# Twelve short fp32 dummy matmuls for six long ones at the start, and one expert-weight load moved behind the last eb loads (Fourier layer and soft MoE, one core)

## The chip, the cores and the metric

The kernel runs on one core of a Trainium2 chip. The metric is device time in microseconds, the median of several runs. Names of engines: PE is TensorE's matrix engine and PEld its weight loading, DVE VectorE, ACT ScalarE, POOL GpSimd, SP SyncE, which here only issues DMAs.

## What is computed

Input `x` is 8 sequences of 2496 tokens with 256 features. A Fourier layer with soft thresholding is followed by a soft mixture of 8 experts with 4 slots each, all in fp32:

```python
X = np.fft.rfft(x, axis=1); Xr, Xi = X.real, X.imag
Yr = Xr @ w_r - Xi @ w_i + b_r
Yi = Xr @ w_i + Xi @ w_r + b_i
Yr = np.sign(Yr) * np.maximum(np.abs(Yr) - 0.01, 0)     # Yi alike
y = np.fft.irfft(Yr + 1j * Yi, n=2496, axis=1).reshape(19968, 256)

logits = y @ phi                                        # phi 256 x 32
d = softmax(logits, over the 19968 tokens)
slot_input = (d.T @ y).reshape(8, 4, 256)
slot_out[e] = np.maximum(slot_input[e] @ w1[e], 0) @ w2[e]   # w1 256 x 1024, w2 1024 x 256
out = softmax(logits, over the 32 slots) @ slot_out
```

## The kernel before

The transforms are matmuls with constant matrices, in two factors of the sequence length. A batch (one of 8 sequences) goes through short groups on PE (pa and px for the forward transform, pk and py for the complex weights, pt, pr and further ones behind the threshold), and its dispatch logits, weights and slot sums follow some groups later. The whole program is written by generators in a heap: each yields a time, and what is due first is written first. Times of the tail are relative to `TB` (function `at`). What is written goes onto its engine in that order: `sp()` (L243) issues a DMA from SP, `aq()` from ACT's queue, `mm()` (L249) and `tr()` (L634) write matmuls and transposes on PE, and each keeps program order. A helper's line is thus the line of many instructions.

**The head.** While the first inputs travel (`xf`, which holds transform constants and the first rows, and the `x` tiles), PE runs dummies: a tile `warm` of zeros, 128x128, multiplied into the PSUM tile `wps`, which nothing reads (L293 to L297). It is an F32R tile, an fp32 form in which a matmul is a single pair of weight load and matmul here. Behind them `head()` (L450) writes the q matmuls (`q_mm`, L394), plain fp32, whose results are copied to `at` and `atr`. The layer's weights come as `wri`, of which POOL and ACT derive sums and differences (`wsum`, `wdh`).

**The tail.** For batch 7 `last_chain()` (L1040) does what the other batches have behind them already: `pg` gives dispatch logits, which ACT copies to `g_sb` and sends to the DRAM tile `gd` (`aq`); SP reads them back in another layout as `gp` (`sp`), and PE multiplies them into `L` (`pL`). Then come the dispatch weights: `ed` is their DRAM tile, `eb` what is read back from it, for batch 6 as for batch 7, and `pd` the slot sums. The combine's logits are read back as `cin` from `c_dr` (`c_load`, L1161), split to `chl` on POOL (`c_prep`), and multiplied by `pc` on PE (`c_trans`, L1180). The experts run in between: `mlp1` with `w1`, `mlp2` with `w2` into `po` (L1222 to L1246). In the last stage `pq` makes the result, ACT and DVE copy it to `ost`, and SP sends it out (L1297 to L1336).

**The expert weights.** 32 matrices of 512 KB (16 of `w1`, 16 of `w2`) have no room of their own. The table `PLAN["T_"]["wl"]` (L156) lists for each, in order, when it is loaded and into which room: `load_w` (L933) takes the next matrix of `wlist`, so that the i-th entry is the i-th matrix. Rooms are tiles whose first use is over: `r`, `a`, `q`, `sm`, `xs` in the chain's pools, `t` one of the `ta_tile` tiles, `h` half an `hl` tile, `hx` one tile more, `T` two of the transposed tiles. `x` is a pair of half matrices (128x512 each), one in a tile of tag `xth` and one of tag `xtl`; each tag has three buffers (`chain_bufs`, L207). Each half is one DMA of SP.

Of the kernel before, what the change touches and what calls it, by code (L numbers as in the profile page):

```python
# [12 lines left out]
F32 = mybir.dt.float32  # L13
F32R = mybir.dt.float32r
# [40 lines left out]
def _constants():  # L55
# [97 lines left out]
    "ko": 0.915,  # L153
    "to": 0.7,
    "late": {'6': {'cms': [11.5, 19.69, 854.1, 854.2, 854.2, 854.2], 'eb': 21.015, 'pt': ['pl', 'pf'], 'de': 0.005, 'pd': [30.6, 30.61], 'pr': [31.55, 31.6, 31.65, 31.7, 31.75], 'pL': [6.05, 6.5], 'pm': 8.05, 'mo': 0.1, 'pb': 9.05, 'eo': 0.4, 'pe': [11.1, 11.5], 'pg': [0.875, 1.275], 'fr': {'sinv': 0, 'm2': 0, 'f1': 0, 'suni': 0}}, '5': {'cms': [14.3, 14.8, 15.6, 20.0, 20.8, 21.5], 'pg': [1.1, 1.8], 'pL': [6.5, 7.2], 'pm': 8.52, 'de': 0.68, 'mo': 0.1, 'pb': 9.05, 'eo': 0.1, 'fr': {'sinv': 1, 'm2': 1, 'f1': 1, 'suni': 0}, 'pe': [11.35, 12.35], 'pp': [12.05, 12.6], 'pd': [18.9, 19.3], 'pr': [40.2, 40.21, 40.22, 40.23, 40.24]}, '4': {'pr': [18.4, 20.49, 24.49, 28.49, 32.49]}},
    "T_": {'wl': [[-45, 'r'], [-44, 'r'], [-43, 'r'], [-31.0, 't'], [-30.7, 't'], [-29.4, 't'], [-27.6, 't'], [-27.8, 't'], [-25, 'q'], [-23.5, 'q'], [-11, 'a'], [-10.3, 'a'], [-9.6, 'a'], [-9.45, 'sm'], [-9.4, 'xs'], [-8.31, 'x'], [-8.3, 'x'], [-8.29, 'x'], [1.07, 'h'], [1.07, 'h'], [13.55, 'h'], [13.55, 'h'], [13.55, 'h'], [13.55, 'h'], [13.55, 'hx'], [13.61, 't'], [13.61, 't'], [13.61, 't'], [13.61, 't'], [13.61, 't'], [13.7, 'T'], [13.7, 'T']], 'cl': 1.02, 'cp': 46.5, 'ct': 46.6, 'du': [[-4.5, 0], [-2.4, 0], [1.2, 0]], 'd1': [5, 2, 4, 0, 0, 0], 'cm': [19.9, 19.91, 19.92, 25, 25.1, 25.2], 'cm7': [0.1, 0.12, 0.3, 0.4, 1, 1], 'ye': 0.2, 'te': [[5.6, 0.2], [5.5, 0.4]], 'pg': [-7, -6.4965, -6.458], 'yt': 0.5, 'wr': -30.6, 'tp': {-2: [0, 0.9, 1.05, 1.05], -1: [-2.4975, -2.497, -2.46, -2.459]}, 'tt': [[[-6.4605, -6.44], -0.3, -0.25, -0.2, [-6.5, -6.4585]], [0.6, 0.7, 0, 0, 0], [12, 11.45, 12.2, 12.3, 12.4]], 'tg': {(7, 0): ('pt', 'ps'), (5, 4): ('ps', 'pl'), (5, 0): ('pl', 'ps')}, 'eg': {(6, 2, 1): 'A', (6, 4, 0): 'V', (6, 4, 1): 'A'}, 'z': 13.55, 'th': [0.1, 0.12], 'tl': [0.2, 0.25]},  # L156
    "f1": [1.5, 2.4],
    "ap1": 1.9,
    "f0": 0.2,
# [29 lines left out]
def fourier_soft_moe_kernel(ctx: ExitStack, tc: tile.TileContext, t: dict, out: bass.AP):  # L189
# [21 lines left out]
    def psum(tag, name):  # L211
        return pp.tile([128, 512], F32, tag=tag, name=name, bufs=psum_bufs[tag])

    def wtile(shape, dt, tag, name):
        if tag == "rte":
            return wqp.tile(list(shape), dt, tag=tag, name=name, bufs=2)
        if tag in a_bufs:
            return wap.tile(list(shape), dt, tag=tag, name=name, bufs=a_bufs[tag])
        if tag in main_bufs:
            return wmp.tile(list(shape), dt, tag=tag, name=name, bufs=main_bufs[tag])  # L220
        return wcp.tile(list(shape), dt, tag=tag, name=name, bufs=chain_bufs[tag])

    x = t["x"]
# [6 lines left out]
    V, A, P = (_InOrder(tc, e) for e in (nc.vector, nc.scalar, nc.gpsimd))  # L230
# [18 lines left out]
    def mm(**kw):  # L249
        tc.keep_in_program_order(nc.tensor.matmul(**kw))  # L250
# [39 lines left out]
        x0.append([xf[:P1, Q1 + e * D : Q1 + e * D + D] for e in range(GP)])  # L290
        pools["f1x"] = xf[:P1, :Q1].rearrange("p (c a r) -> p c a r", c=2, r=R)

    warm = wtile([128, 128], F32R, "k1", "warm")  # L293
    P.memset(warm.bitcast(F32), 0.0)
    wps = psum("ps", "wps")
    for _ in range(6):
        mm(out=wps, lhsT=warm, rhs=warm.unsqueeze(1).broadcast_to([128, 4, 128]), start=True, stop=True)  # L297

    while len(x0) < G // GP:
        load_x0()  # L300
# [11 lines left out]
    xs = wtile([128, 6 * KS], F32R, "xs", "xs")  # L312
# [721 lines left out]
    T_ = PLAN["T_"]  # L1034
# [173 lines left out]
    rhs = []  # L1208
# [98 lines left out]
    for j in range(NBLK):  # L1307
# [6 lines left out]
        if not pqs:  # L1314
            pqs = [(k, psum(("pf", "pl")[k % 2], f"pq{k}")) for k in ((0, 1) if j == 0 else (j,))]
            for a in range(2):
                for k, pq in pqs:
                    lo = k * TR - k * TR % F
                    mm(
                        out=pq,  # L1320
                        lhsT=cts[lo][:, k * TR - lo : k * TR - lo + TR],
                        rhs=rhs[a].rearrange("p b d -> p (b d)"),
                        start=(a == 0),
                        stop=(a == 1),
# [4 lines left out]
        if j + 1 == starts[i] + OUTS[i]:  # L1329
            n = OUTS[i] * 512  # L1330
            sp(
                out=out[128 * 512 * starts[i] : 128 * 512 * (j + 1)].rearrange("(p f) -> p f", p=128),
# [68 lines left out]
```

## Time and profile before

| | us |
|---|---|
| runs | 517.89, 517.67, 515.95 |
| median | 517.67 |
| profiled execution, its own time | 516.78 |
| span of that execution, first to last instruction | 515.0 |
| PE busy in the span | 500.7 (97%) |
| DVE, ACT, POOL busy | 405.7, 312.6, 296.2 |
| result leaves (last stage) | from 461.89 on |

The span is a little shorter than the time of the execution that it belongs to; the rest lies before the first and behind the last instruction. Matmuls are pipelined, so that the busy time of PE is the time in which some matmul is under way. What stood still and for whom is read from the timeline, where a row has the idle time ahead of it and what ended that, and from the chain of work that ended last. The DMA share counts the time of packets on the 16 DMA engines; queue q1 holds SP's DMAs, q10 ACT's, q8 the fetches of PE's instructions.

### The profile page before, as it was taken

What the parts mean: (1) busy time and instruction counts of PE and PEld (TensorE: products, weight loads), DVE (VectorE), ACT (ScalarE), POOL (GpSimd) and SP (SyncE); (2) the same over time, 40 slices, a digit from 0 to 9 for tenths busy, and PEclk for the clock granted to TensorE, in tenths of its full rate; (3) what the DMA queues carried; (4) which work ended last, traced back from release to release, by engine and by line L of the source; (5) the groups of instructions that cost most, each with busy time, mean ns of one, the idle gap of its engine ahead of it and who ended that gap; (6) DMA issues with size and microseconds to landing.
All of it is one profiled execution on the core that took longest, in us unless ns stands there. A gap on an engine that the chain in (4) does not pass through costs nothing.

```text
span 515.0 us, 11951 instructions
## 1 busy us (share of the span) xinstructions
PE 500.7 (97%) x4475; PEld 440.1 (85%) x4475; DVE 405.7 (79%) x776; ACT 312.6 (61%) x704; POOL 296.2 (58%) x280
## 2 busy tenths in 40 slices
PE   8999999999999999999999999999999999999992
PEld 7889999999999999998999898889899878468881
DVE  2897787799968898889889988897898866257661
ACT  2776666777676766676667666655534446138761
POOL 0686786768676757675667577867475503153310
PEclk9999999999999999999999999999999999999997
DMA  8655555675665657565656566696685567959998
GB/s 299 229 186 185 182 171 201 177 242 149 257 181 183 165 194 203 175 167 201 188 174 174 211 186 207 163 307 182 242 256 150 199 163 194 410 198 403 408 419 342
DMA packets 87485, 114.91 MB, mean 223 GB/s; under 512 B 46191, under 2 KB 65119, under 8 KB 85891
## 3 DMA queue, kind: packets, MB, share of 16 engines
q1 hardware_dynamic: 86860, 113.65, 66.5%
q8 instruction: 35, 0.57, 0.5%
q10 hardware_dynamic: 567, 0.50, 0.3%
q14 instruction: 23, 0.19, 0.1%
HBM read 66.78 MB, written 47.34 MB: 222 GB/s over the span
## 4 chain that ended last, share of the span: by engine, by line
PE 84%; DMA 6%; DVE 4%; POOL 1%; ACT 1%; issue 1%; SPq 1%; DVEq 0%; ACTq 0%; POOLq 0%
PE py L250 21%; PE px L250 13%; PE pk L250 10%; PE pa L250 10%; PE pq L250 9%; PE pt L634 6%; PE pr L250 3%; PE pe L250 2%; PE pc L1186 2%; PE pL L250 2%; PE pg L250 2%; PE pd L250 1%; PE hps L250 1%; DMA out<-ost 1%; DMA gp<-gd 1%; DMA wri<-in_w 1%
## 5 line engine op out<-in xcount | busy, mean ns | idle before, releaser
L185 POOL TENSOR_TENSOR xs<-xsm,xs 128x256 fp32r<-128x256 f32 x77 | 63.3, 823 | 96.4 <-DVE xs L185 66.3
L185 POOL TENSOR_TENSOR rt<-ut,rt 128x512 f32<-128x512 f32 x79 | 104.7, 1326 | 15.1 <-DVE rt L185 13.8
L185 POOL TENSOR_TENSOR xl<-xr,xh 117x512 fp32r<-117x512 f32 x72 | 97.7, 1357 | 12.9 <-ACT xh L185 12.9
L250 PE MATMUL px<-smov,ap 128*128 128x128 f32 x640 | 85.1, 276 | 0.1
L250 PEld LDWEIGHTS px<-smov,ap 128*128 128x128 f32 x640 | 80.3, 192 | 4.8 <-DVE xsm L185 0.3
L185 DVE SCALAR_TENSOR_TENSOR ut<-py,pk,k 128x256 f32<-128x256 f32 x160 | 69.5, 475 | 11.7 <-PE py L250 11.0
L185 ACT CAST xth<-px 128x512 fp32r<-128x512 f32 x80 | 46.9, 587 | 43.6 <-PE px L250 21.6
L185 ACT COPY ast<-pa 128x512 f32<-128x512 f32 x75 | 44.2, 589 | 46.1 <-PE pa L250 46.1
L185 DVE TENSOR_TENSOR xtl<-px,xth 128x512 fp32r<-128x512 f32 x80 | 54.6, 683 | 18.6 <-ACT xsm L185 18.6
L250 PE MATMUL pk<-xs,w_rh 128*128 128x256 f32 (+1 forms) x320 | 66.1, 290 | 0.1
L185 DVE TENSOR_SCALAR rt<-ut 128x512 f32<-128x512 f32 x69 | 65.5, 949 | 0.6
L250 PE MATMUL py<-xth,nwsh 128*128 128x256 f32 (+1 forms) x160 | 53.2, 333 | 0.1
L250 PEld LDWEIGHTS pk<-xs,w_rh 128*128 128x128 f32 x320 | 51.9, 189 | 0.9 <-DVE xs L185 0.6
L185 ACT CAST xh<-xr 117x512 fp32r<-117x512 f32 x75 | 47.4, 635 | 0.4 <-DMA xr<-in_x 0.4
L634 PE MATMUL pt<-pk,rt 128*128 128x128 f32 x320 | 45.2, 274 | 0.0
L250 PE MATMUL py<-xth,wdh 128*128 128x256 f32 (+1 forms) x160 | 44.8, 280 | 0.0
L250 PE MATMUL py<-xtl,nwsh 128*128 128x256 f32 (+1 forms) x160 | 44.6, 279 | 0.0
L250 PE MATMUL py<-xtl,wdh 128*128 128x256 f32 (+1 forms) x160 | 44.5, 278 | 0.0
L250 PE MATMUL py<-xth,wdl 128*128 128x256 f32 (+1 forms) x160 | 44.5, 278 | 0.0
L250 PE MATMUL py<-xth,nwsl 128*128 128x256 f32 (+1 forms) x160 | 44.4, 278 | 0.0
L250 PE MATMUL pk<-xs,w_rl 128*128 128x256 f32 (+1 forms) x160 | 44.4, 278 | 0.0
L185 ACT COPY T<-pt 128x512 f32<-128x512 f32 x66 | 39.2, 601 | 6.8 <-PE pt L634 5.1
(197 smaller groups left out, 1192.3 us busy)
## 6 DMA issues: line engine op xcount, KB each, us to landing
xr<-in_x SPq DMA_DIRECT2D x35, 512.0 KB
ap<-adr SPq DMA_DIRECT2D x70, 256.0 KB
adr<-ast SPq DMA_DIRECT2D x21, 768.0 KB
out<-ost SPq DMA_DIRECT2D x12, 1024.0 KB
w<-in_moe_w SPq DMA_DIRECT2D x21, 512.0 KB
out<-ost SPq DMA_DIRECT2D x14, 512.0 KB
hl<-in_moe_w SPq DMA_DIRECT2D x6, 512.0 KB
x<-in_x SPq DMA_DIRECT2D x10, 256.0 KB
```

Of the source, the lines that this page charges most:

```text
L185: return lambda *a, **k: self.tc.keep_in_program_order(f(*a, **k))
L250: tc.keep_in_program_order(nc.tensor.matmul(**kw))
L634: tc.keep_in_program_order(nc.tensor.transpose(out=out, in_=in_, identity=identity))
L1186: nc.tensor.transpose(out=pc[:, i * P1 : (i + 1) * P1], in_=chls[b][x][:, 2 * (r + i) : 2 * (r + i) + 2].rearrange("p g h s -> p (g h s)") ...
```

## The change

It has two parts. In the head `warm` is a plain F32 tile, and twelve matmuls of 64 columns are written where six of 512 were. In the table the third `x` entry leaves its place at -8.29 (the 18th entry) and a new one stands at 13.56, behind `hx` (the 25th). As entries are matched to matrices by place, the matrices 17 to 24 change rooms with that: 17 and 18 go to `hl` halves, 19 to 22 to the next `hl` halves, 23 to `hx`, 24 to the `x` pair; the others keep theirs.

```diff
-    "T_": {'wl': [ ... [-8.31, 'x'], [-8.3, 'x'], [-8.29, 'x'], [1.07, 'h'], [1.07, 'h'], [13.55, 'h'], ... [13.55, 'hx'], [13.61, 't'], ...
+    "T_": {'wl': [ ... [-8.31, 'x'], [-8.3, 'x'], [1.07, 'h'], [1.07, 'h'], [13.55, 'h'], ... [13.55, 'hx'], [13.56, 'x'], [13.61, 't'], ...
...
-    warm = wtile([128, 128], F32R, "k1", "warm")
-    P.memset(warm.bitcast(F32), 0.0)
+    warm = wtile([128, 128], F32, "k1", "warm")
+    P.memset(warm, 0.0)
     wps = psum("ps", "wps")
-    for _ in range(6):
-        mm(out=wps, lhsT=warm, rhs=warm.unsqueeze(1).broadcast_to([128, 4, 128]), start=True, stop=True)
+    for _ in range(12):
+        mm(out=wps[:, :64], lhsT=warm, rhs=warm[:, :64], start=True, stop=True)
```

On PE, at the program's start, this is the row of matmuls before; `q_0` and `q_1` are the first two PSUM tiles of `q_mm`, and an fp32 matmul, one row here, is two pairs in the trace:

```order
L1397 UNCONDITIONAL_BRANCH
L250 MATMUL wps<-warm 128x512 x6
L250 MATMUL q_0_150<-xf 128x2x20x3 x2
L250 MATMUL q_1_153<-xf 128x2x20x3 x2
L250 MATMUL q_0_150<-xf,x_2_89 128x2x20x3 x2
```

and with the change:

```order
L1397 UNCONDITIONAL_BRANCH
L250 MATMUL wps<-warm 128x64 x12
L250 MATMUL q_0_156<-xf 128x2x20x3 x2
L250 MATMUL q_1_159<-xf 128x2x20x3 x2
L250 MATMUL q_0_156<-xf,x_2_95 128x2x20x3 x2
```

The number of dummies and their size differ; what follows on PE is the same.

On SP, at the old place of the third `x` load (at 411 us in the trace), before: `w_0` and `w_1` are the two halves of a matrix, `ed` the dispatch weights of batch 6, `gp` the logits of batch 7 read back:

```order
L244 DMA w_0_6241<-in_moe_w 128x512
L244 DMA w_1_6242<-in_moe_w 128x512
L244 DMA w_0_6249<-in_moe_w 128x512
L244 DMA w_1_6250<-in_moe_w 128x512
L244 DMA ed_6256<-ea_6169 120x704
L244 DMA gp_6417<-gd_6271 40x22x32 x2
L244 DMA gp_6417<-gd_6271 40x20x32
```

and with the change:

```order
L244 DMA w_0_6247<-in_moe_w 128x512
L244 DMA w_1_6248<-in_moe_w 128x512
L244 DMA ed_6258<-ea_6175 120x704
L244 DMA gp_6419<-gd_6273 40x22x32 x2
L244 DMA gp_6419<-gd_6273 40x20x32
```

One pair of halves is gone ahead of `ed`.

On SP, at the new place, before (`eb` of batch 7, then the `hl` halves, `hx` as the first `w`, and the first of the five loads into `ta_tile` tiles):

```order
L244 DMA eb_6627<-ed_6498 64x20x32 x2
L244 DMA hl_6632<-in_moe_w 128x1024 x2
L244 DMA hl_6635<-in_moe_w 128x1024 x2
L244 DMA w_6638<-in_moe_w 128x1024
L244 DMA w_6650<-in_moe_w 128x1024
```

and with the change:

```order
L244 DMA eb_6629<-ed_6500 64x20x32 x2
L244 DMA hl_6634<-in_moe_w 128x1024 x2
L244 DMA hl_6637<-in_moe_w 128x1024 x2
L244 DMA w_6640<-in_moe_w 128x1024
L244 DMA w_0_6652<-in_moe_w 128x512
L244 DMA w_1_6653<-in_moe_w 128x512
L244 DMA w_6656<-in_moe_w 128x1024
```

The two halves stand between `hx` and the `ta_tile` loads. The order on DVE, ACT and POOL is the same; on PE the `mlp2` matmuls of the shifted matrices read other tiles.

## Rows read from the trace of the kernel before

**Rows 1.** The page, parts 1, 3, 4: engines; a queue; chain shares

```profile
PE 500.7 (97%) x4475; PEld 440.1 (85%) x4475; DVE 405.7 (79%) x776; ACT 312.6 (61%) x704; POOL 296.2 (58%) x280
...
q8 instruction: 35, 0.57, 0.5%
...
PE 84%; DMA 6%; DVE 4%; POOL 1%; ACT 1%; issue 1%; SPq 1%; DVEq 0%; ACTq 0%; POOLq 0%
```

**Rows 2.** Windows: us, PE, PEld, DVE, ACT, POOL, PEclk, DMA share, GB/s

```profile
460.00:462.00 2.00, 1.72 (x8) 1.42 (x8) 1.06 (x3) 0.92 (x3) 1.09 (x1) 1.00 0.04 8
...
464.00:466.00 2.00, 2.00 (x13) 1.65 (x12) 1.78 (x4) 1.75 (x5) 1.50 (x2) 1.00 1.03 410
```

**Rows 3.** Timeline, head: start us, us, instruction, count [idle before <-releaser]

```profile
0.99 2.93 PE L250 MATMUL wps<-warm 128*128 128x512 f32 x6 [0.99 <-POOL warm L185]
...
4.46 1.15 PE L250 MATMUL q<-xf 117*128 117x120 f32 x8 [0.54 <-DMA xf<-in_xf]
...
6.63 7.22 PEld L250 LDWEIGHTS q<-xf,x 117*128 117x128 f32 x64 [0.31 <-DMA x<-in_x]
...
16.48 0.62 ACT L185 CAST wdh<-wri 128x512 fp32r<-128x512 f32 x1 [0.35 <-POOL wri L185]
```

**Rows 4.** Chain of work that ended last, the head: start us, us, what

```profile
7.93 5.43 DMA wri<-in_w
...
22.39 0.70 PE pa L250 x3
```

**Rows 5.** Windows, columns as in rows 2: PE behind pL

```profile
424.86:441.70 16.84, 16.81 (x187) 12.87 (x184) 11.06 (x24) 9.15 (x20) 5.33 (x10) 1.00 0.80 245
```

**Rows 6.** Timeline of SP's DMA issues, about 411 us

```profile
410.82 0.37 SPq L244 DMA_DIRECT2D w<-in_moe_w  x1
411.29 0.38 SPq L244 DMA_DIRECT2D w<-in_moe_w  x1
411.76 0.39 SPq L244 DMA_DIRECT2D ed<-ea  x1
```

**Rows 7.** DMA queues: packets, MB, share; 413 to 415, then 415 to 417

```profile
q1 hardware_dynamic: 304, 0.59, 85.8%
q10 hardware_dynamic: 2, 0.00, 0.4%
...
q10 hardware_dynamic: 403, 0.31, 46.5%
...
q8 instruction: 1, 0.02, 3.0%
```

**Rows 8.** Chain of work that ended last, 415 to 424 us

```profile
415.85 2.83 DMA gd<-g_sb
...
419.74 3.58 DMA gp<-gd
```

**Rows 9.** Timeline of PE, 420 to 425 us

```profile
421.22 1.97 PE L634 MATMUL pt<-pk,rt 128*128 128x128 f32 x16
423.45 1.41 PE L250 MATMUL pL<-gp,pk 120*117 120x352 f32 x4 [0.26 <-DMA gp<-gd]
```

**Rows 10.** Timeline of SP's DMA issues: three of the five last cin reads

```profile
449.20 0.33 SPq L244 DMA_DIRECT2D cin<-c_dr  x1
450.51 0.30 SPq L244 DMA_DIRECT2D cin<-c_dr  x1
...
452.50 0.30 SPq L244 DMA_DIRECT2D cin<-c_dr  x1
```

**Rows 11.** Timeline of all engines, 454 to 463 us

```profile
454.91 3.64 PE L250 MATMUL po<-w,z 128*32 128x256 f32 x64
...
456.82 0.62 POOL L185 CAST chl<-cin 117x512 fp32r<-117x512 f32 x1
...
461.89 1.17 SPq L244 DMA_DIRECT2D out<-ost  x2
...
462.25 0.56 PE L1186 MATMUL pc<-pk,chl 117*128 117x117 f32 x4
```

More of the change, by code (lines that the diff above doesn't have):

```diff
@@ L155 @@
     "late": {'6': {'cms': [11.5, 19.69, 854.1, 854.2, 854.2, 854.2], 'eb': 21.015, 'pt': ['pl', 'pf'], 'de': 0.005, 'pd': [30.6, 30.61], 'pr': [31.55, 31.6, 31.65, 31.7, 31.75], 'pL': [6.05, 6.5], 'pm': 8.05, 'mo': 0.1, 'pb': 9.05, 'eo': 0.4, 'pe': [11.1, 11.5], 'pg': [0.875, 1.275], 'fr': {'sinv': 0, 'm2': 0, 'f1': 0, 'suni': 0}}, '5': {'cms': [14.3, 14.8, 15.6, 20.0, 20.8, 21.5], 'pg': [1.1, 1.8], 'pL': [6.5, 7.2], 'pm': 8.52, 'de': 0.68, 'mo': 0.1, 'pb': 9.05, 'eo': 0.1, 'fr': {'sinv': 1, 'm2': 1, 'f1': 1, 'suni': 0}, 'pe': [11.35, 12.35], 'pp': [12.05, 12.6], 'pd': [18.9, 19.3], 'pr': [40.2, 40.21, 40.22, 40.23, 40.24]}, '4': {'pr': [18.4, 20.49, 24.49, 28.49, 32.49]}},
-    "T_": {'wl': [[-45, 'r'], [-44, 'r'], [-43, 'r'], [-31.0, 't'], [-30.7, 't'], [-29.4, 't'], [-27.6, 't'], [-27.8, 't'], [-25, 'q'], [-23.5, 'q'], [-11, 'a'], [-10.3, 'a'], [-9.6, 'a'], [-9.45, 'sm'], [-9.4, 'xs'], [-8.31, 'x'], [-8.3, 'x'], [-8.29, 'x'], [1.07, 'h'], [1.07, 'h'], [13.55, 'h'], [13.55, 'h'], [13.55, 'h'], [13.55, 'h'], [13.55, 'hx'], [13.61, 't'], [13.61, 't'], [13.61, 't'], [13.61, 't'], [13.61, 't'], [13.7, 'T'], [13.7, 'T']], 'cl': 1.02, 'cp': 46.5, 'ct': 46.6, 'du': [[-4.5, 0], [-2.4, 0], [1.2, 0]], 'd1': [5, 2, 4, 0, 0, 0], 'cm': [19.9, 19.91, 19.92, 25, 25.1, 25.2], 'cm7': [0.1, 0.12, 0.3, 0.4, 1, 1], 'ye': 0.2, 'te': [[5.6, 0.2], [5.5, 0.4]], 'pg': [-7, -6.4965, -6.458], 'yt': 0.5, 'wr': -30.6, 'tp': {-2: [0, 0.9, 1.05, 1.05], -1: [-2.4975, -2.497, -2.46, -2.459]}, 'tt': [[[-6.4605, -6.44], -0.3, -0.25, -0.2, [-6.5, -6.4585]], [0.6, 0.7, 0, 0, 0], [12, 11.45, 12.2, 12.3, 12.4]], 'tg': {(7, 0): ('pt', 'ps'), (5, 4): ('ps', 'pl'), (5, 0): ('pl', 'ps')}, 'eg': {(6, 2, 1): 'A', (6, 4, 0): 'V', (6, 4, 1): 'A'}, 'z': 13.55, 'th': [0.1, 0.12], 'tl': [0.2, 0.25]},
@@ new lines @@
+    "T_": {'wl': [[-45, 'r'], [-44, 'r'], [-43, 'r'], [-31.0, 't'], [-30.7, 't'], [-29.4, 't'], [-27.6, 't'], [-27.8, 't'], [-25, 'q'], [-23.5, 'q'], [-11, 'a'], [-10.3, 'a'], [-9.6, 'a'], [-9.45, 'sm'], [-9.4, 'xs'], [-8.31, 'x'], [-8.3, 'x'], [1.07, 'h'], [1.07, 'h'], [13.55, 'h'], [13.55, 'h'], [13.55, 'h'], [13.55, 'h'], [13.55, 'hx'], [13.56, 'x'], [13.61, 't'], [13.61, 't'], [13.61, 't'], [13.61, 't'], [13.61, 't'], [13.7, 'T'], [13.7, 'T']], 'cl': 1.02, 'cp': 46.5, 'ct': 46.6, 'du': [[-4.5, 0], [-2.4, 0], [1.2, 0]], 'd1': [5, 2, 4, 0, 0, 0], 'cm': [19.9, 19.91, 19.92, 25, 25.1, 25.2], 'cm7': [0.1, 0.12, 0.3, 0.4, 1, 1], 'ye': 0.2, 'te': [[5.6, 0.2], [5.5, 0.4]], 'pg': [-7, -6.4965, -6.458], 'yt': 0.5, 'wr': -30.6, 'tp': {-2: [0, 0.9, 1.05, 1.05], -1: [-2.4975, -2.497, -2.46, -2.459]}, 'tt': [[[-6.4605, -6.44], -0.3, -0.25, -0.2, [-6.5, -6.4585]], [0.6, 0.7, 0, 0, 0], [12, 11.45, 12.2, 12.3, 12.4]], 'tg': {(7, 0): ('pt', 'ps'), (5, 4): ('ps', 'pl'), (5, 0): ('pl', 'ps')}, 'eg': {(6, 2, 1): 'A', (6, 4, 0): 'V', (6, 4, 1): 'A'}, 'z': 13.55, 'th': [0.1, 0.12], 'tl': [0.2, 0.25]},
```

## The prediction

> **What bounds the kernel now.** I read the page first [rows 1]: PE is busy 500.7 of 515.0 us and holds 84% of the chain of work that ended last, DMA 6%. Then the windows of the last stage [rows 2]: from 464 us on the 16 DMA engines are busy all the time (share 1.03, about 410 GB/s) and PE has 13 matmuls in 2 us to keep up with it. The last 50 us are thus set by the output, which cannot start before the combine's first matmuls, and these stand behind PE's work of the first 460 us. Just before, at 460 to 462, the DMA share is 0.04: no backlog stands in front of the output. A microsecond saved or lost on PE before 460 therefore moves the end by the same microsecond; one on a transfer counts only where PE waits for it. The profiled execution took 516.78 us, 1.78 more than its span; the median of the three runs is 517.67. I make the sum against 516.78 and put its difference onto the median.
>
> **The dummies.** Before, six matmuls of 512 columns run from 0.99 to 3.92 us; the engine then waits for the DMA of xf, and the first q starts at 4.46 [rows 3]. Removed: 6 pairs of weight load and matmul. Added: 12 fp32 matmuls, and an fp32 matmul is two pairs here (the four matmuls of the first q's are eight records [rows 3]), so 24 pairs of 64 columns. The trace does not show such a pair at the head, so I bound it. The dummies of before took 2.93/6 = 0.49 us, their starts 0.43 apart; a 512-column matmul at 22.39 takes 0.70/3 = 0.23 [rows 3, 4]. The head thus runs at about half the later rate, the lower of the two levels (1.2 and 2.4 GHz), and the page's granted clock, an average over 13 us there, decides nothing against these durations. At the higher level a pair of 32 columns takes 3.64/64 = 0.057 us (po [rows 11]) and one of 120 columns 7.22/64 = 0.113 (q [rows 3]). Doubled for the lower level, a pair of 64 columns lies between 0.114 and 0.226 us: 24 of them are 2.7 to 5.4 us, and they end between 3.7 and 6.4. By columns between the two (0.057 + 32/88 x 0.056 = 0.077, doubled 0.155) it is 3.7 us, and they end at 4.7. I take an end between 3.7 and 4.7, as columns and weight rows of a pair overlap in both rows.
>
> What of a later end counts? Up to 4.46 nothing, since xf isn't there. PE waits another 0.31 us at 6.63 for the DMA of x, and ACT 0.35 us at 16.48 for POOL's wri [rows 3], which stands behind the landing of wri at about 13.4 in the chain [rows 4]; a delay of PE's q's is swallowed by the first, and the step behind wri has 0.35 more. So an end at 4.7 costs nothing, the worst end of 6.4 costs 1.94 - 0.31 - 0.35 = 1.3 us. Below nothing it cannot go: no earlier dummy lets the first q start before xf has landed. **Term: 0, bounds 0 to +1.3.** DVE, ACT and POOL keep their order; the memset of `warm` has the same size.
>
> PE's stream grows by 18 pairs, 36 instructions of some 9000, and shifts where its code is fetched: queue 8 moved 0.57 MB in 35 packets [rows 1], about one of 16 KB per 256 PE instructions. The fetches come some 36 instructions earlier, at the mean rate 36 x 500.7/8950 = 2 us. One of them lies in 415 to 417 [rows 7], and holds 3.0% of 16 engines for 2 us, that is 0.96 us on one engine. A transfer spread over all engines lands with its last one, so a fetch can cost or give up to 1 us to whichever transfer it meets. This is a bound of both signs, not a term.
>
> **The load taken away from its old place.** The third x entry is the last two of SP's row of 128x512 weight DMAs, at 410.82 and 411.29; ed of batch 6 follows at 411.76 [rows 6]. Without them ed is issued about 0.9 us earlier, and 512 KB less stand before batch 7's transfers. What a load of 512 KB costs in a full queue is seen later: the cin reads are released each by an older landing, 449.20 and 450.51, which is 1.31 us for 512 KB [rows 10]. Behind the old place stand gd, batch 7's dispatch logits written out by ACT's queue, and gp, read back by SP. The queues by window [rows 7]: from 413 to 415 SP's queue q1 holds 85.8% of the engines and ACT's q10 moves 2 packets, from 415 to 417 q10 moves 403. So gd moves when the loads have drained, and 1.3 us less of them lets it go up to 1.3 us earlier. In the chain [rows 8] the last gd is issued at 415.85 and takes 2.83 us, gp then 3.58, and pL starts at 423.45. But PE is not idle meanwhile: pt runs until 423.19, and pL waits 0.26 us for gp [rows 9]. PE's order is fixed, so with gp at least 0.26 earlier pL starts right behind pt and not sooner. From 424.86 to 441.70 PE is busy 16.81 of 16.84 us [rows 5], with eb(7), pd(7) and the hl weights in that stretch arriving in time; the 0.26 gained is carried through as long as nothing in it was just in time. Next late would then be PE itself. **Term: -0.26, bounds 0 to -0.26**: gd may gain what the loads hold it up, at most 1.3 us, of which 0.26 is wanted; its last piece is issued at 415.85 whatever the loads do, so that it may also gain nothing.
>
> The Trainium skill, "DMA: Bandwidth & Descriptors", section "Queues, rings and completion order", says that each DMA engine goes round the queue rows that have work, a packet at a time. By it gd would not stand behind SP's loads at all but share the engines with them from 413 on, the term would be 0 and the sum 517.7. The trace's 2 packets against 403 speak against it in this place, if the time from issue to the first packet is not what kept q10 empty.
>
> **The load at its new place.** The two halves now follow hx, behind eb(7) and the four hl loads. Everything behind in SP's row comes 512 KB later, 1.3 us: the five loads into ta_tile, the two into T, then the five cin reads of 447.93 to 452.50 [rows 10]. The weights' last user is the second matrix of the experts: po runs 64 pairs at 454.91 to 458.55 [rows 11], the last 16 of them, for the two weights in T, from 454.91 + 48 x 0.057 = 457.6. These two are four halves, issued just ahead of cin; each cin is released by the transfer eight places ahead, so that the fifth, at 452.50, tells when the first of the four halves has landed. Three more at 1.31/2 = 0.65 us give 454.4, one more for an engine that lags 455.1; after the change 455.7 to 456.4. That leaves at least 1.2 us to spare up to 457.6, of at least 2.5 before. The first cin feeds chl on POOL at 456.82, with up to 0.75 us of delay, in pieces of which the first takes 0.62 us; pc needs chl at 462.25 [rows 11], 5.4 us after. The DMA engines run empty at 460 [rows 2], so the 1.3 us of traffic is gone before the output needs them. **Term: 0**; with its cover gone it would cost what the delay exceeds 1.2 us more. A wait of SP for the room adds none: the x rooms' halves were free at 411 already.
>
> **Sum:** 0 - 0.26 + 0 = -0.26, so 516.78 becomes 516.5 for a run like the profiled one, and the median 517.67 becomes 517.4.
>
> **Rivals.**
> A. Nothing moves. gp lands when it did, as gd's 2.83 us are fixed time or a fetch on one engine, not the loads' queue. For it: 403 packets move within 2 us behind an issue at 413.10, and a delay of some 2 us between issue and first packet would look the same; the rule of round-robin. Against: q1's 85.8% just then. 516.8, median 517.7.
> B. The clock rises later (slower). The dummies of before kept the columns flowing without a break; 24 short pairs have gaps at every weight load, and if PE's clock is granted by what the engine did, the q's may begin at the lower level. Each q pair then costs 0.113 us more. If they stay low as long again as the dummies took up to the first q (4.46 - 0.99 = 3.47 us, 15 pairs of 0.226), 15 x 0.113 = 1.7 us are lost, less 0.31 and 0.35: +1.1, with the gain +0.8 to the median, 518.5; with a late end of the dummies on top up to 519.5. It decides from the sixth low pair on (0.66/0.113). For it: the head's low rate is a fact of the rows. Against: the sum of column passes is the same (6 x 512 = 12 x 64 x 4, by the eight records and two passes that q's 0.113 us for 120 columns suggests).
> C. The same, with at least 29 low pairs of the 88 (29 x 0.113 - 0.66 = 2.6 us): slower by over 0.5%, 520.3 to 527.
> D. Late weights (slower too). The two weights in T land over 1.2 us later than reckoned, and po waits. One fetch on one engine (0.96 us) isn't enough, two (1.92) cost 0.7: 518.1.
> E. A fetch of PE's code moves off the last output transfers and lets them end up to 1 us sooner: 516.4.
>
> The Trainium skill, "TensorE: Matmul & The Clock Gate", section "Part 1: The HAM clock gate", has PE start throttled and be released by its activity; the rows of the head agree as far as the lower rate goes, and no run here shows yet whether 64-column fp32 pairs release it as well.
>
> **How the numbers follow.** Main case 0.59; A 0.14; B 0.14; C 0.05; D 0.02; E 0.03; something that I don't see, and that is faster, 0.03. About 0.5% (2.6 us: below 515.1, above 520.3) is what a measurement of this kernel can tell from no change. Main, A, D, E and all of B but 0.01 lie within it: same 0.91. Slower is C with that tail of B: 0.06. Faster would take 2.6 us, more than the gains named, 0.26 and 1, together: 0.03, the unseen case. Range: the main case and A carry the scatter of the runs, 515.95 to 517.89 before, so 515.7 below; above it takes in B at 518.5 and a little of the late end, 518.8.
>
> **What would show it.** In the head: 24 dummy pairs ending by 4.7, the first q at 4.46, 0.113 us per pair; a q at twice that is B or C, and its count the loss. At 411: ed directly behind the second x load, gd's packets ahead of 415, gp's landing before 423.1 and no idle time before pL; an idle time of 0.26 still there is A. Behind hx two more halves, cin's issues 1.3 us later, no idle time within po's 64; one there is D. First output at 461.6. I am wrong if pL gains 0.26 and the output does not start earlier: then something in 425 to 460 was just in time.

## The result and the profile after

The changed kernel takes 520.45 us (median of 8 runs, 519.35 to 522.43) against 517.62 us (median of 8 runs, 515.16 to 518.87) in the same sessions: **slower, ratio 1.007, 95% interval 1.0055 to 1.0085**, which is 2.8 to 4.4 us. The forecast was 517.4 with a range up to 518.8, and a time that can't be told from no change.

The profiled execution of the changed kernel took 519.85 us with a span of 518.1, against 516.78 and 515.0: 3.07 us more. These are lines of parts 1 and 4 of its page, to be held against [rows 1]:

```profile
PE 504.4 (97%) x4493; PEld 444.8 (86%) x4493; DVE 404.4 (78%) x776; ACT 312.6 (60%) x704; POOL 295.7 (57%) x280
...
PE 91%; DMA 3%; DVE 3%; ACT 1%; issue 0%; SPq 0%; DVEq 0%; POOL 0%; ACTq 0%; POOLq 0%
```

There are 18 more matmul records (24 dummies for 6) and 3.7 us more of busy PE, and the chain is even more PE's: 91% for 84%. DMA lost its share because no transfer stands on the chain in the head or before batch 7's pL any longer. The first lines of the timeline say where the time went (start us, us, engine, line, instruction, count, idle time before it and what ended that; they answer to [rows 3]):

```profile
0.99 5.38 PE L250 MATMUL wps<-warm 128*128 128x64 f32 x24 [0.99 <-POOL warm L185]
...
6.17 2.01 PE L250 MATMUL q<-xf 117*128 117x120 f32 x8
...
7.97 9.02 PE L250 MATMUL q<-xf,x 117*128 117x120 f32 x72
...
18.98 0.61 ACT L185 CAST wdh<-wri 128x512 fp32r<-128x512 f32 x1
```

Three things are to be seen. From the first dummy to the first q 5.18 us pass, 0.216 for each of the 24 pairs; before it was an xf wait that let the first q go at 4.46, now it is PE itself, at 6.17. The first eight q's take 2.01 us where they took 1.15. And the brackets of [rows 3] are gone: q no longer waits for x, nor wdh for wri; both waits are swallowed. The windows of the changed kernel (us, busy us and number of PE, PEld, DVE, ACT, POOL, clock, DMA share, GB/s) show how long the q's stay slow:

```profile
4.00:6.00 2.00, 2.00 (x12) 2.00 (x11) 0.00 (x0) 0.00 (x0) 0.00 (x0) 1.00 0.92 320
...
7.00:8.00 1.00, 1.00 (x7) 1.00 (x7) 0.00 (x0) 0.00 (x0) 0.00 (x0) 1.00 1.02 367
...
9.80:11.00 1.20, 1.20 (x13) 1.20 (x12) 0.65 (x2) 0.24 (x1) 0.00 (x0) 1.00 1.06 405
```

A window's count (x7, x13) is of the matmuls under way in it. Five of them start between 7 and 8 us, ten in the 1.2 us from 9.8 to 11. PE is busy all the time in either; a pair starts 0.214 us behind the one before it up to about 9.7 us, and 0.112 behind it from then on. These are the two levels of TensorE's clock, 1.2 and 2.4 GHz, and the trace's record of the granted clock has its first entry at the full level at 9.67. The column PEclk prints 1.00 in all three lines: it has no entry to show ahead of 9.67, so here the steps decide, not the column. Before, that entry stood at 4.23, ahead of the first q.

The same matmul in both traces, followed along PE's order, gives the whole account:

| matmul | before | after | later by |
|---|---|---|---|
| first q | 4.46 | 6.17 | 1.71 |
| pa at the start of batch 1's steady part | 44.67 | 47.50 | 2.83 |
| py of a middle batch | 270.37 | 273.30 | 2.93 |
| pk, behind a pL of batch 5 that waits | 318.65 | 322.12 | 3.47 |
| pg of batch 7 | 415.24 | 418.74 | 3.50 |
| pt behind pL of batch 7 | 427.30 | 430.36 | 3.06 |
| pc behind the last po | 463.69 | 466.97 | 3.28 |
| last pq | 504.38 | 507.42 | 3.04 |

The head costs 2.83 us, and nothing after it costs that much. The tail did what the second half of the change was made for. The first line is SP's issue of gp before; the others, against [rows 6, 8, 9], are of the changed kernel: ACT's issue of gd's last piece, SP's issues of gp, and PE's pL:

```profile
418.81 2.88 SPq L244 DMA_DIRECT2D gp<-gd  x4
...
419.34 0.33 ACTq L247 DMA_DIRECT2D gd<-g_sb  x1
...
420.94 2.79 SPq L244 DMA_DIRECT2D gp<-gd  x4
...
426.58 1.35 PE L250 MATMUL pL<-gp,pk 120*117 120x352 f32 x4
```

gp is issued 1.60 us behind gd's last piece, where it was 2.96 (415.85 to 418.81), and pL waits for nothing. The last 70 us, against [rows 10, 11], have cin's first issue, the last po and the first output:

```profile
451.93 5.41 SPq L244 DMA_DIRECT2D cin<-c_dr  x5
...
460.85 0.57 PEld L250 LDWEIGHTS po<-w,z 128*32 128x32 f32 x10 [0.18 <-DMA w<-in_moe_w]
...
465.18 4.31 SPq L244 DMA_DIRECT2D out<-ost  x5
```

The po of the last weights did wait here, 0.18 us.

### The profile page after: what moved, and what is told of

Same layout as the page of the kernel before. It is cut to its first block, busy times and chain, and to the rows that moved or that the text cites. A ratio compares the mean times of both kernels' runs of the same rounds, so it can differ in the third digit from the quotient of the medians.

```text
span 518.1 us, 11990 instructions
## 1 busy us (share of the span) xinstructions
PE 504.4 (97%) x4493; PEld 444.8 (86%) x4493; DVE 404.4 (78%) x776; ACT 312.6 (60%) x704; POOL 295.7 (57%) x280
## 4 chain that ended last, share of the span: by engine, by line
PE 91%; DMA 3%; DVE 3%; ACT 1%; issue 0%; SPq 0%; DVEq 0%; POOL 0%; ACTq 0%; POOLq 0%
PE py L250 21%; PE px L250 13%; PE pk L250 10%; PE pa L250 10%; PE pq L250 9%; PE pt L634 7%; PE pr L250 4%; PE q L250 2%; PE pe L250 2%; PE pc L1186 2%; PE pL L250 2%; PE pg L250 2%; PE pd L250 1%; PE po L250 1%; PE hps L250 1%; DMA out<-ost 1%
```

## The experiments

**Theory H (the head).** 24 short pairs take 0.214 us each and so hold up the first q by 1.71 us, and the clock rises only when the q's have run for some us; the moved load is worth 0.4 us. **Rival T (the table).** The delay of the head is swallowed further on and the moved load costs. A later question within H is this: is it fp32, the number of pairs or the short columns that keep the clock low?

### The two halves apart

The head alone, `e1_head`, is the changed kernel with the old table (the entry that moves):

```diff
-[13.56, 'x'], ...
+[-8.29, 'x'], ...
```

> The twelve short fp32 dummies alone, the table of loads as before. Theory H (the head): 24 pairs cost 0.214 us each at the lower clock level and end at 6.4 us, the first q starts at 6.17 instead of 4.46, and the clock still rises only some 3.5 us into the q's, after 17 of them: the first xs matmul behind the head 2.8 us later than before, and the end 2.8 to 3.3 us later (about 520.6). pL of batch 7 still waits for gp. Theory T (the table is what costs): the head's delay is swallowed further on, and this kernel takes 517.7.

Measured: 519.73 against 516.80 us, ratio 1.0063 (1.0048 to 1.0079).

The table alone, `e2_table`, is the changed kernel with the six F32R dummies of 512 columns:

```diff
-    warm = wtile([128, 128], F32, "k1", "warm")
...
+    warm = wtile([128, 128], F32R, "k1", "warm")
...
-    for _ in range(12):
-        mm(out=wps[:, :64], lhsT=warm, rhs=warm[:, :64], start=True, stop=True)
+    for _ in range(6):
+        mm(out=wps, lhsT=warm, rhs=warm.unsqueeze(1).broadcast_to([128, 4, 128]), start=True, stop=True)
```

> The moved load alone, six long dummies as before. Theory H: head as before (first q at 4.46, clock full), pL of batch 7 no longer waits (0.3 to 0.4 us won at 423), the last eight po wait some 0.2 us for the last weight: 517.2 to 517.7. Theory T: 520 or more.

Measured: 515.76 against 516.80 us, ratio 0.9982 (0.9971 to 0.9993): faster than before, a little more than expected, and po does not wait in its trace. T falls: the head alone makes the kernel slower, the table alone makes it faster. The ratios add up to +0.45%, and the two together gave 0.7 (0.55 to 0.85) and 0.58 (0.38 to 0.79, `e12_after` below).

In the trace of the head alone the clock's first full entry comes at 11.87, not at 9.67, although PE's instructions up to there are the same, and the steady part runs 3.89 us later than before, not 2.83. So the loss of the head differs between executions, by half a microsecond for each that the clock is late:

```profile
6.17 2.01 PE L250 MATMUL q<-xf 117*128 117x120 f32 x8
7.97 10.07 PE L250 MATMUL q<-xf,x 117*128 117x120 f32 x72
```

The 72 q records take 10.07 us here and 9.02 in the changed kernel.

### What holds up the clock

Six short dummies, `e3_six_short` (`range(6)` for `range(12)`, old table), end before xf lands, so that no q is late:

> Six fp32 dummies of 64 columns instead of six long ones, table as before: 12 pairs that end at 0.99 + 12 x 0.214 = 3.6 us, before xf is there. So no q is late, and only the clock is left. If short fp32 pairs count for nothing with the clock, it rises some 3.5 us after the first q, at about 8.0, after 16 q's at 0.102 us more each: 1.65 us, less the waits of 0.31 and 0.35 that were there: 1.0 to 1.3 us slower, about 518.8. If the clock only needs PE to have begun work at 0.99, it rises at 4.2 as before and the time is 517.6. If it rises at a time that depends on all work since 0.99, at 9.67 as with twelve dummies, 24 q's are low: 1.8 to 2.1 us slower.

Measured: 519.02, ratio 1.0046 (1.0032 to 1.0061). The trace has the first q at 3.80, the clock up at 8.29 and the steady part 0.97 us later than before: the head did what the first case said. The time is worse than that by more than a microsecond (2.2 us for 1.0 to 1.3). In the traced execution, the slowest of the six at 519.92, pL waited about 1.0 us in batch 5 and 1.28 us in batch 7 (below), which the head doesn't explain; what the median has beside the head is not shown.

No dummies at all (`e5_none`, the lines of `warm` and `wps` left out):

> No dummies at all, table as before. The q's begin when xf has landed (3.8 to 4.5 us) at the lower level. If the short pairs did nothing for the clock, this is the kernel with six short dummies again: clock up 4 to 6 us after the first q, some 20 q's at 0.214 us, 1.0 to 1.6 us slower than before in the head, 518 to 519. If the short pairs did bring the clock on, it rises later than there: 2 us or more.

Measured: 517.62 against 517.04, ratio 1.0018 (1.0004 to 1.0033). First q at 3.73, clock up at 8.09, steady part 0.85 us late. That is less than was expected. Six short fp32 dummies thus brought the clock up no earlier than none did, in one trace each, and by the times none is a little better than six (1.0018 for 1.0046) and clearly better than twelve (1.0063).

Then three kernels that set the causes apart, all with the old table. 24 F32R pairs of 128 columns, `e4_f32r_24`:

```diff
-    for _ in range(6):
-        mm(out=wps, lhsT=warm, rhs=warm.unsqueeze(1).broadcast_to([128, 4, 128]), start=True, stop=True)
+    for _ in range(24):
+        mm(out=wps[:, :128], lhsT=warm, rhs=warm, start=True, stop=True)
```

> 24 F32R dummies of 128 columns: as many pairs as the twelve fp32 dummies make, as many columns in all as the six long ones (3072), table as before. If what matters is columns in time, a pair takes 0.107 us, they end at 3.6 and the clock rises at 4.2: 517.6. If a pair costs 0.214 us whatever its columns, they end at 6.1 and q starts 1.6 us late; with the clock up by then 0.9 to 1.3 us slower, with the clock late as well 2.8 slower.

Measured: 520.77, ratio 1.0078 (1.0062 to 1.0095). First q at 6.17, clock up at 12.25. The pairs take what the fp32 ones of 64 columns take, and the clock is later still, so that the loss is 4.0 us where 2.8 was the worst expected: it isn't plain fp32 that keeps it low.

Twelve F32R pairs of 256 columns, `e9_f32r_12` (`wps[:, :256]`, `rhs` broadcast to 2 x 128):

> Twelve F32R dummies of 256 columns, table as before: the same columns in all as six of 512 or 24 of 128, in 12 pairs. If a pair costs 0.214 us at the lower level up to 256 columns, they end at 3.6 as the six short fp32 ones do, with the same number of pairs. If the number of weight loads or their share keeps the clock low, it rises at 8 or later: 1 us slower. If what counts is columns run in that time, the clock rises at 4.2 as before: 516.8.

Measured: 517.08 against 517.04, ratio 1.0005 (0.9990 to 1.0020). They end at 3.9 us, as the six of 512 do, since a pair starts 0.213 us behind the one before it: no more than with 128 columns. The first q is at 3.72, the clock up at 6.94 and the steady part 0.26 us late. The kernel before itself had 6.61 and 0.40 in its second trace (`e13_before`), so this is as good as the old head. Against six short fp32 dummies it has the same 12 pairs in the same time; the columns are more, and F32R, and the time is 1.0005 for 1.0046.

Three plain fp32 dummies of 512 columns (6 pairs), `e6_fp32_512`, with `warm` as in the changed kernel, whose head the edit is shown against:

```diff
-    for _ in range(12):
-        mm(out=wps[:, :64], lhsT=warm, rhs=warm[:, :64], start=True, stop=True)
+    for _ in range(3):
+        mm(out=wps, lhsT=warm, rhs=warm.unsqueeze(1).broadcast_to([128, 4, 128]), start=True, stop=True)
```

> Three fp32 dummies of 512 columns (6 pairs), table as before. If an fp32 pair takes its columns at the rate of an F32R one, they end at 3.9 as before and it is told whether plain fp32 itself keeps the clock low: with columns as the cause the clock rises at 4.2 and the time is 516.8; with fp32 as the cause it rises at 8 or later, 1 us slower or more. If an fp32 pair takes two cycles a column, they end at 6.1 and the first q is 1.7 us late, with the clock up: 1.0 us slower.

Measured: 517.70 against 517.04, ratio 1.0008 (0.9992 to 1.0025). The clock is up at 4.34, while they still run:

```profile
0.99 4.49 PE L250 MATMUL wps<-warm 128*128 128x512 f32 x6 [0.99 <-POOL warm L185]
5.32 1.05 PE L250 MATMUL q<-xf 117*128 117x120 f32 x8
```

These pairs start 0.853 us apart at the lower level, twice the 0.427 of the six F32R ones, and 0.43 apart behind 4.34. The first q is at 5.32, 0.86 us later than before, but at the full level: eight in 1.05 us. The steady part is 0.27 us late. So behind long matmuls the clock was up early in plain fp32 as in F32R, and behind short ones late in either.

Twelve fp32 dummies of 16 columns, `e10_fp32_16` (`[:, :16]` for `[:, :64]`, old table), for the price of a pair:

> Twelve fp32 dummies of 16 columns, table as before. If a pair's floor at the lower level is its weight load of 128 columns, the 24 pairs take 0.214 us each as with 64 and with 128 columns, end at 6.4, and the first q starts at 6.17: 519.5 to 521. If columns count, a pair of 16 columns takes less than half of that, the dummies end before xf lands, and the head is that of the kernel with six short dummies: 517.5 to 519.

There is one execution, of 521.17 us, and its trace:

```profile
0.99 5.30 PE L250 MATMUL wps<-warm 128*128 128x16 f32 x24 [0.99 <-POOL warm L185]
6.13 2.04 PE L250 MATMUL q<-xf 117*128 117x120 f32 x8
```

(6.13 - 0.99)/24 = 0.214 us for a pair of 16 columns, of 64 and of 128 alike. With the F32R pairs of 256 columns (0.213 us) that makes four widths at one price. The columns are hidden in a pair's floor; what these pairs have in common is the weight load of 128 columns, and what else is fixed in a pair. The clock is up at 12.67, the latest of all.

All traces of the head together; "late" is the steady part (pa at 44.67 in the first trace of before) against that trace:

| dummies | kernels | first q | clock full | late |
|---|---|---|---|---|
| 6 F32R pairs of 512 | before, its second trace, table alone, x at 1.08 | 4.46, 3.71, 3.83, 3.72 | 4.23, 6.61, 4.28, 4.62 | 0, 0.40, -0.59, -0.74 |
| 12 F32R pairs of 256 | e9 | 3.72 | 6.94 | 0.26 |
| 6 fp32 pairs of 512 | e6 | 5.32 | 4.34 | 0.27 |
| none | e5 | 3.73 | 8.09 | 0.85 |
| 12 fp32 pairs of 64 | e3 | 3.80 | 8.29 | 0.97 |
| 24 fp32 pairs of 64 | after, its second trace, head alone, e11 | 6.17, 6.16, 6.17, 6.16 | 9.67, 9.63, 11.87, 11.59 | 2.83, 2.82, 3.89, 3.77 |
| 24 F32R pairs of 128 | e4 | 6.17 | 12.25 | 4.06 |
| 24 fp32 pairs of 16 | e10 | 6.13 | 12.67 | 4.26 |

The mean of the four with the changed head is 3.33 us, of the four with the old one -0.23: the head is worth 3.6 us. The trace of before had the latest first q of all kernels whose dummies end in time; xf landed later in that execution, which the forecast took for granted.

### Where the third load is put

The load at 1.08, behind the two hl loads that stand ahead of ed of batch 7, with the six long dummies, `e8_x_108`:

```diff
-[1.07, 'h'], [1.07, 'h'], ... [13.55, 'hx'], [13.56, 'x'], [13.61, 't'], ...
+[1.07, 'h'], [1.07, 'h'], [1.08, 'x'], ... [13.55, 'hx'], [13.61, 't'], ...
```

> Six long dummies as before; the third x load is neither at its old place nor behind hx but right behind the two hl loads that stand before ed of batch 7 (at 427 us in the trace of before). pL of batch 7 doesn't wait, as in the kernel with the table alone (0.3 to 0.5 us won), and the last weights come no later than before, so po doesn't wait and cin is not late: 515.5 to 516.5. Rival: the load is still under way when ed and eb of batch 7 are wanted, eb lands late and pd waits up to 1 us: 517 to 518.

Measured: 515.96 against 517.04, ratio 0.9978 (0.9966 to 0.9990), from the table alone (0.9971 to 0.9993) not to be told apart. Both are faster than the kernel before, and so than the changed one. The rival of that expectation, a wait behind the moved load, is not seen: the pt behind pL is 0.99 us earlier than in the trace of before, and pc behind the last po 1.03, so nothing waited in between.

The same table with the changed kernel's head, `e11_short_x108`:

> Twelve short fp32 dummies as in the changed kernel, with the third x load at 427 us (behind the two hl loads ahead of ed of batch 7) and not behind hx. The head costs what it did; gp is issued 1.6 to 1.8 us behind the last gd and pL doesn't wait; the last weights come 1.3 us sooner than in the changed kernel, so the 0.2 us of po's wait there are gone if that wait belongs to the place. About 520, 0 to 0.4 us less than the changed kernel.

Measured: 519.39 against 516.83, ratio 1.0049 (1.0029 to 1.0069). No po waits for a weight.

The changed kernel and the kernel before once more, `e12_after` and `e13_before`, unedited:

> The changed kernel once more, for a second trace of it. First q at 6.17 whatever xf does; the clock rises at another time than 9.67 (it was 11.87 with the same head in another execution), between 9 and 12.5, and each us more costs half a us; po waits for the last weight again if that is no accident. 520 to 521.

Measured: 519.99, ratio 1.0058 (1.0038 to 1.0079). The clock is up at 9.63, as in the first trace of this kernel and against the expectation, and po does not wait this time, so that its wait was that one execution's.

> The kernel before once more, for a second trace of it. If the landing of xf at 4.46 was that one execution's, the first q starts at 3.7 to 3.9 here, as in four other traces with dummies that end by then, and the head runs 0.5 to 0.75 us earlier than in the trace of before; pL waits between 0 and 1.7 us for gp. 516.5 to 517.7.

Measured: 516.79 against 516.83, ratio 1.0000 (0.9985 to 1.0016). First q at 3.71, as expected; but the head runs 0.40 us later, not earlier, since the clock is up only at 6.61.

From all fourteen traces, the tail:

| third load | gd's last issue to gp's first, us | idle before pL of batch 7, us | pL to cin's first issue, us |
|---|---|---|---|
| old place: before, its second trace, e1, e3, e4, e5, e6, e9, e10 | 2.96, 3.07, 2.24, 3.52, 1.80, 4.51, 2.58, 2.44, 2.79 | 0.26, 0.23, 0, 1.28, 0, 1.74, 0, 0, 0.48 | 24.48, 24.73, 23.87, 24.07, 24.08, 24.12, 24.08, 23.97, 24.38 |
| behind hx: after, its second trace, e2 | 1.60, 1.60, 1.70 | 0, 0, 0 | 25.35, 25.39, 25.48 |
| at 1.08: e8, e11 | 1.79, 1.60 | 0, 0 | 23.87, 24.07 |

The two longest of the nine waits of the old place, from the timeline of the kernel without dummies and then of that with six short ones:

```profile
425.74 1.41 PE L250 MATMUL pL<-gp,pk 120*117 120x352 f32 x4 [1.74 <-DMA gp<-gd]
```

```profile
426.79 1.41 PE L250 MATMUL pL<-gp,pk 120*117 120x352 f32 x4 [1.28 <-DMA gp<-gd]
```

With the load ahead of them gd and gp take 2.88 us on the mean from the one issue to the other, without it 1.66: 1.2 us less, wherever the load goes. The idle time at pL was 0.44 us on the mean of the nine, and none in the five. The stretch from the first pg of batch 7 to the pt behind pL, which also has what the idle time leaves out, took 12.21 us on the mean of the nine (11.56 to 13.53) and 11.62 in each of the five: 0.59 us less. Behind hx the load makes cin 1.2 us later (25.4 against 24.2 on the mean), at 1.08 not at all (24.0); no time is seen to come from that, but for the 0.18 us of po in one trace of three.

## Why the prediction was wrong

The step that failed is the term of the dummies, put at 0 with bounds of 0 to +1.3. In the traces of the changed head it was 2.8 to 3.9 us. Two things in it were wrong: the price of a pair, and the clock.

**The price of a pair.** The bounds were 0.114 and 0.226 us; the runs showed 0.214 to 0.216, close to the upper one, and the choice was 0.155, from columns between po's row and q's. That choice went wrong in two ways. po's 0.057 us [rows 11] is no price of one pair of 32 columns: 32 are the columns of its weights, each po moves 256, and `mlp2` issues four of them whose 32 output rows each stand side by side. Each record lasts 0.38 us and they start 0.057 apart on the mean, so that they overlap. And a pair with a weight load of 128 columns has a floor: 16, 64 and 128 columns gave the same 0.214 us at the lower level, and q's 120 columns too. The right neighbour was q, doubled (0.226), with nothing taken off for fewer columns. An end of the dummies by 4.7 us was forecast, and they end at 6.4: the first q is 1.71 us late, less 0.66 swallowed as reckoned, which is 1.05 us of the loss. It was inside the bounds of the term (0 to +1.3), and the range up to 518.8 would have covered it alone. That an end up to 4.46 costs nothing was true of the one trace only: in the six others whose dummies end by then, or that have none, the first q starts at 3.71 to 3.83 (e6's dummies end too late to tell).

**The clock.** Rival B had the mechanism: the q's begin at the lower level. Its chance (0.14, with C's 0.05) was too small, and the term had nothing for it. The forecast had 15 low pairs in B; the changed kernel had (9.67 - 6.17)/0.214 = 16.4, and up to 30.6 came in the other traces with 24 short pairs. 16.4 x 0.102 us (0.214 for 0.112) are 1.67 us. With the late end, 1.71 + 1.67 - 0.31 - 0.35 = 2.72 us against 2.83 measured, and less 0.44 at pL 517.67 + 2.83 - 0.44 = 520.1, where 520.45 was measured. The same sum, with each trace's own first q and clock entry, falls short of the measured delay by 0.07 to 0.16 us in all ten traces in which it is above zero, six with the 24 pairs and four with other dummies or none. So the late start and the low level are all of the head's loss but these 0.16 us at most.

The two have the same cause, short pairs, and so come together. The prediction did add them, but wrongly: "up to 519.5". B's sum (1.0 us, written as 1.1) had spent the 0.31 and 0.35 already, so that the worst end of 6.4 adds all its 1.94 us to 518.5, which is 520.4. The forecast's own terms thus came to the measured time (in part by luck, 1.94 where 1.71 was measured, 15 low pairs where there were 16.4), and the range left them out.

B's reason, gaps at every weight load, is not to be read from the profile's busy time: PE is busy without a break from 0.99 on (2.00 of 2.00 us in the window above), while the clock stays at its lower level for 8.7 us. The steps show it: a pair of 128 F32R columns takes the 0.214 us of one of 256, so that its columns fill half of that at most. The argument against B was the sum of column passes, the same before and after. The runs refute it: 6 x 512, 12 x 256 and 24 x 128 columns in F32R are the same sum, and the clock was up at 4.2 to 6.6, at 6.9 and at 12.3.

The Trainium skill, "TensorE: Matmul & The Clock Gate", section "Part 1: The HAM clock gate (the 'warmup' mystery)", says that the throttled state is the default and activity releases it. The traces agree with the default: all fourteen begin at the lower level (0.214 us for a pair of up to 128 columns, 0.427 for an F32R one of 512). They agree with the release in so far as each reaches the full level behind PE's first work; but behind 24 pairs without a gap, in 5.2 us, it came at 9.6 to 12.7 us, behind six long F32R matmuls, in 2.9 us, at 4.2 to 6.6. Counted from the first q, it came 4.4 us behind it with no dummies at all, and 3.5 to 6.5 us behind it with 24 short pairs.

**The 0.31 and 0.35 us** that x and wri give back were right; both brackets are gone in the changed kernel.

**The load at its old place.** Right in mechanism and sign. -0.26 was the term, with 0.26 as its bound because pL waited that long in that one trace; the changed kernel gained 0.44 there (3.50 to 3.06 in the table of the first section), more than the idle time. From the start of the last pt to that of pL 0.535 us passed before, and 0.109 in the changed kernel: an unhindered pL starts long before the pt ahead of it ends, so that an idle time counted from that end leaves out part of the wait. The bound was wrong twice: it took that idle time for the size, and one execution's for all. The same wait was 0 to 1.74 us in nine traces, 0.44 on the mean, and the stretch around it 0.59 longer than without the load. The gain by gd, "up to 1.3 us", measured 1.2. What was said of the queues held. The first line is of the 1.5 us behind gd's first issue before (413.10), the others of the 1.5 us behind the same issue in the changed kernel (416.60):

```profile
q1 hardware_dynamic: 223, 0.42, 84.9%
...
q1 hardware_dynamic: 121, 0.29, 65.1%
q10 hardware_dynamic: 88, 0.13, 23.6%
```

Before, ACT's q10 moves nothing in that time; in the changed kernel it moves 88 packets. In the nine traces with the load ahead it moves 0 to 3 packets and its first one comes 1.36 to 2.11 us behind the issue; in the five without it moves 68 to 110, and the first comes after 0.84 to 0.97. So the 2 us from issue to packet, which rival A took for fixed, are not. The rule of "DMA: Bandwidth & Descriptors" in the Trainium skill ("Queues, rings and completion order"), that an engine goes round the queue rows with work, does not bring the term to 0, against what the prediction drew from it in rival A. Packets of both queues do move within the same 1.5 us in the changed kernel (121 and 88), but none of gd's did while q1 held 84.9% of the engines. What held them up there is not shown.

**The load at its new place.** 1.3 us of delay for cin were forecast, 1.2 measured (25.4 for 24.2 behind pL), and that it costs nothing held in two of three traces. In the third the last po waited 0.18 us. Rival D named that wait; it was smaller than D's 0.7.

**Rival A** (nothing moves) fell with e2 and e8, **rival E** was not seen: the end moved with PE's last matmul, 3.04 later for 3.07.

**What stays open.** Why the clock rises at 9.6 in two executions of the changed head and at 11.6 and 11.9 in two others, with the same instructions on PE up to there, was not tried and stays open, as do 4.23 and 6.61 in two executions of the kernel before. Nor is it settled why pL of batch 5 waited in four of fourteen traces (0.54 us in the changed kernel, near 310 us): its gp landed late there, in kernels with either head and with either place of the load. The time of the table alone is 0.9 us less than before (0.4 to 1.5), with the load at 1.08 1.1 us less (0.5 to 1.8), more than the 0.59 us of the stretch around pL; the intervals hold that too.

## What to carry to other kernels

Price dummies by what the first real matmul then costs, in its start and in its rate: here long ones (256 or 512 columns) were followed by a full clock at 4.2 to 6.9 us, short ones at 8.3 to 12.7, none at 8.1. A matmul with a full weight load has a floor per pair: below it, here from 128 columns down, fewer columns saved nothing, so count pairs, and read the floor from the nearest pair that loads as many weights, not from matmuls that run side by side. When two costs have one cause, add them in full before drawing the range. And when a gain is bounded by an idle time, read that idle time in several executions: 0.26 us in one trace was 0 to 1.74 in nine.

## What was not expected of the hardware

At the lower clock level a pair with a weight load of 128 columns took 0.214 us for 16, 64 or 120 columns in plain fp32 and for 128 or 256 in F32R; at the full level q's pair of 120 took 0.112. A pair of 512 columns took 0.853 us in plain fp32 and 0.427 in F32R, both at the lower level. Back-to-back short pairs kept PE busy and left the clock low until 9.6 to 12.7 us from the start of the span, longer than no dummies at all (8.1). And the rise moved from one execution to the next: 4.2 and 6.6 us with one program, 9.6 to 11.9 with the same PE instructions up to there. A 192 KB write on ACT's queue moved no packet for 1.4 to 2.1 us behind its issue while loads stood in SP's queue, and for 0.8 to 1.0 us when 512 KB less stood there.
